# Attention, soft mixture and gated layer on one core: where the products of the score maxima stand, and when the dispatch chain runs

## The chip, the cores and the metric

One core of one Trainium2 chip runs the kernel. The metric is the device time of one execution in microseconds (us). Five engines work side by side, each on its own queue in program order: TensorE (PE; its weight loads are shown as PEld), VectorE (DVE), ScalarE (ACT), GpSimd (POOL), and SyncE (SP), which issues the DMAs. They wait for each other by semaphores.

## What is computed

```python
# attention: B=4, H=8, S=1152, D=64; queries pooled in pairs
q_pool = q.reshape(B, H, S // 2, 2, D).mean(axis=3)
scores = (1 / sqrt(D)) * q_pool @ k.T
scores -= scores.max(-1)
attn = exp(scores); attn /= attn.sum(-1) + 1e-9
out = attn @ v                       # laid out as x: 2304 tokens x 512
# soft mixture: 8 experts of 4 slots
logits = x @ phi
d = exp(logits - logits.max(0)); d /= d.sum(0) + 1e-9     # dispatch, over tokens
slot_input = d.T @ x                 # then two layers with relu per expert
c = exp(logits - logits.max(1)); c /= c.sum(1) + 1e-9     # combine, over slots
x = c @ slot_out
# gated layer: rms norm, silu(xn @ w_gate) * (xn @ w_val) @ w_out
```

All of it is in float32; the products of scores use a split of q and k into a rounded and a low part.

## The kernel before

The attention goes in 16 pairs of heads (`p`), each over nine key tiles `kt` of 128 keys, with the 576 pooled queries in two halves `h`. For one key tile and half, `qk` (lines 366 to 380) writes a score tile into PSUM with eight matmuls (high k by high q, low k by high q, high k by low q, and minus the row maxima), and ScalarE turns it into an `e` tile with an exponential. `add_e` sums the `e` tiles on GpSimd (`acc`), for the softmax's denominator. `av` multiplies by the values. The pairs 0 and 15 (`HALVED`) take their halves one after the other; the middle pairs 1 to 14 take both halves in each key tile.

The row maxima of the next pairs come from products of their own (`max_item`, lines 315 to 332): two matmuls of rounded q and k into a PSUM tile `mxp`, and a reduction on VectorE. A pair has twelve such items and two shorter ones (`max_tail`). `max_red` joins them, `max_row` transposes (`mxt`) and copies them negated (`mrow`), `send_row` moves them by DMA to `mr`, which the scores of the next pair use.

Score tiles, `mxp` tiles and all tiles of the side work share one PSUM tag with three slots of two banks (`two_banks`, line 225; `bank` takes a slot too). A tile takes a slot when the reader of an earlier tile has been written into the program and waits on the chip until that reader is done. The values' accumulators have two slots of their own.

The order of the work is written out by hand (lines 823 to 851): for each key tile, the steps of `STEP` run in turn: `q0`, `q1` are the two score tiles, `m` is one item of maxima if the quota of `MAX` allows, `e0`, `e1` are the additions, and `a`, `b`, `c` are the values' products of the three last key tiles, in every third key tile only (`VISIT`). So three key tiles of scores (a stretch) are followed by a visit to the values. The side work of the pair (roundings, low parts, the denominators of the pair before, its division, its logits, the dispatch) has due times in `AT`: the whole part is the key tile, the fraction the place among the steps. Everything goes into the engines' queues in that order.

For the pair before, `sums`, `recips`, `x_turn` (transposes `xo`, line 442), `x_divide` (line 451), `x_logits` (`xl`, line 460), `x_share` (`ls`, line 469) and `logit_add` (`lg`, lines 479, 480) give the normalized x and its logits. Four pairs make a batch: at the end of pairs 4, 8 and 12 `d_turn` transposes the batch's logits (`lgt`, line 497) and takes their maxima (`mm`, line 498), `d_exp` exponentiates them at the start of the pair behind, and `slot_part` and `slot_turn` (`pp`, line 538) follow in it. `low_k` (`kl`, line 310) and `low_q` are the low parts for the next pair, `turn_64` joins two parts of a weight, all on VectorE. After the attention come the experts and the gated layer, which the change doesn't touch.

Of the kernel before, what the change touches and what calls it, by code (L numbers as in the profile page):

```python
# [18 lines left out]
NP = 16  # L19
# [5 lines left out]
TB = 96  # L25
# [2 lines left out]
NG = 6  # L28
NF = 12

STEP = "q0 m q1 m e0 e1 a b c".split()
STEP_0 = "q m m e a b c".split()
VISIT = 3
PART = 5
MAX = [1, 1, 2, 1, 1, 2, 1, 1, 2]
MAX_1 = [2, 2, 2, 2, 2, 2, 1, 1, 2]
AHEAD = 4
AT = dict(
    take_x=0.0,
    load_64=[0.1, 3.0, 5.0],  # L40
# [1 line left out]
    load_k=0.31,  # L42
    spill=[1.4, 4.4],
    sum_q=2.2,
    sums=2.7,
    round_k=[2.72, 5.6],
    abs_64=[2.73, 8.6, 8.61],
    turn_64=[2.66, 5.63, 5.64],
    recips=2.84,
    max_tail=[2.85, 2.86],  # L50
    low_q=2.95,
    max_red=5.6,
    high_q=5.61,
    low_k=[5.65, 8.62],
    max_row=5.8,
    send_row=6.0,
    x_turn=[5.83, 8.83],
    x_divide=[5.84, 8.84],
    block_q=5.9,
    load_v=7.3,  # L60
    x_logits=8.85,
    drop_x=8.855,
    x_share=8.86,
    logit_add=8.87,
    d_turn=8.95,
    d_exp=0.05,
    d_back=2.83,
    d_copy=2.835,
    slot_part=5.82,
    slot_copy=5.95,  # L70
    slot_turn=8.82,
    c_soft=[2.97, 5.66, 8.63],
    load_ew=[1.0, 3.4],
    load_14=[0.7, 1.7, 2.2, 2.7, 3.7, 4.2, 4.7, 5.7, 6.2, 7.7],
    load_15=[0.5, 1, 1.5, 2, 2.5, 3, 3.5, 4, 4.5, 5.5, 5.84, 6, 6.5, 7, 7.5, 8, 8.5],
)
AT_0 = dict(
    round_k1=[1.06, 1.56],
    block_q1=2.6,
    low_k=[1.3, 1.8],  # L80
# [65 lines left out]
def attention_softmoe_gated_kernel(ctx: ExitStack, tc: tile.TileContext, kT, qT, vv, ip, cst, w1, w2, wg, wv, wo, rg, out):  # L146
# [291 lines left out]
    def x_turn(p, js):  # L438

        o = bank([TB, len(js), 128], "xo")  # L440
        for i, j in enumerate(js):
            pe.transpose(out=o[:, i, :], in_=xu[p][:, TB * j:TB * j + TB], identity=ident)  # L442
            xo[p, j] = o, i

    def x_divide(p, js):
        r = rr[p].rearrange("p h t s -> p (h t) s")
        o = xo.pop((p, js[0]))[0]
        for j in js[1:]:
            xo.pop((p, j))
        n, j0 = len(js), js[0]  # L450
        dv.tensor_tensor(out=xts[j0 // 3][:, j0 % 3:j0 % 3 + n, p % 4, :].rearrange("p n (s d) -> p n s d", s=2),
                         in0=o[:, 0:n].rearrange("p n (s d) -> p n s d", s=2),
                         in1=r[:, j0:j0 + n, :, None].to_broadcast([TB, n, 2, 64]), op=ALU.mult)
# [227 lines left out]
    def side(p):  # L681
# [27 lines left out]
        if l >= 0:  # L709
            at("take_x", lambda i: take_x(l))  # L710
            at("sums", lambda i: sums(l))
            at("recips", lambda i: recips(l))
            at("x_turn", lambda i: x_turn(l, range(3 * i, 3 * i + 3)))
            at("x_divide", lambda i: x_divide(l, range(3 * i, 3 * i + 3)))
            at("drop_x", lambda i: rel("B"))
            at("x_logits", lambda i: x_logits(l, range(6)))
            at("x_share", lambda i: x_share(l, range(6)))
            at("logit_add", lambda i: logit_add(l))
            if p % 4 == 0:
                at("d_turn", lambda i: dpart.__setitem__(("d", l // 4), (d_turn(l // 4), d_neg(l // 4))))  # L720
            if p % 4 == 1 and p > 1:
                b = p // 4 - 1
                at("d_exp", lambda i: d_exp(b, *dpart.pop(("d", b))))
                at("d_back", lambda i: d_back(b))
                at("d_copy", lambda i: d_copy(b))
                at("slot_part", lambda i: slot_part(b))
                at("slot_copy", lambda i: slot_copy(b))
                at("slot_turn", lambda i: slot_turn(b, pt[:, b]))
            if p % 4 == 2 and p > 2:
                b = p // 4 - 1  # L730
                at("c_soft", lambda i: (c_max, c_exp, c_soft2)[i](b))
# [26 lines left out]
    with tc.manual_schedule():  # L758
# [64 lines left out]
        for p in range(NP):  # L823
# [2 lines left out]
            steps = [(kt, h) for h in range(2) for kt in range(NKT)] if p in HALVED else [(kt, None) for kt in range(NKT)]  # L826
            for u, (kt, h) in enumerate(steps):
                now = u / 2 if p in HALVED else u
                order = STEP if h is None else STEP_0
                quota = min(sum((MAX_0 if p == 0 else MAX_1 if p == 1 else MAX)[:u + 1]),  # L830
                            0 if p == NP - 1 else 12 - AHEAD if p == NP - 2 else 99)
                for i, step in enumerate(order):
                    while todo and todo[0][0] <= now + i / len(order) / len(steps) * 9:
                        todo.pop(0)[2]()
                    n = int(step[1]) if len(step) > 1 else h
                    if step[0] == "q":
                        qk(p, kt, n)
                    elif step == "m":
                        if mx < quota:
                            next_max(p, mx)  # L840
                            mx += 1
                    elif step[0] == "e":
                        add_e(p, kt, n)
                    elif kt % VISIT == VISIT - 1:
                        k = kt - 2 + "abc".index(step)
                        for x in (0, 1) if h is None else (h,):
                            if p == NP - 1 and x == 1 and k == NKT - 1:
                                sums(p, (1,))
                            av(p, k, x)
# [411 lines left out]
```

## Time and profile before

| | us |
|---|---|
| median of 3 runs | 778.94 |
| range of the runs | 778.91 to 779.56 |
| span of the profiled execution, first to last instruction | 776.2 |
| TensorE busy in the span | 736.0 (95%) |
| VectorE / ScalarE / GpSimd busy | 477.7 / 410.5 / 426.5 |
| mean granted clock of TensorE | 0.984 |

The profiled execution is known by its span; the median of the runs, which also holds what lies around the span, is 2.7 us longer. In the rows of the profile, L375 is line 375 of the kernel; "sc<-qh,kh" names the tile written and the tiles read; "x2" merges neighbours of one kind; in brackets stands how long the engine was idle before, and what released it.

### The profile page before, as it was taken

The numbers are of one execution on the slowest core, as the hardware profiler recorded it, in microseconds if no ns is written. First come the engines' busy times: TensorE is split into PE (matmuls) and PEld (weight loads), VectorE is DVE, ScalarE is ACT, GpSimd is POOL, SyncE is SP. The second block draws the span as 40 slices with busy tenths as digits, with TensorE's granted clock in tenths as the row PEclk, the third lists the DMA queues.
The fourth block names the chain that finished last, engine by engine and source line by source line (L and its number), as shares of the span: only waits on it lengthen the run. The fifth ranks groups of instructions, "written<-read, shape, count | busy, mean of one in ns | idle before, by whom it ended". The sixth has DMA issues, their size and how long they took to land.

```text
span 776.2 us, 15539 instructions
## 1 busy us (share of the span) xinstructions
PE 736.0 (95%) x6143; PEld 508.0 (65%) x6143; DVE 477.7 (62%) x711; ACT 410.5 (53%) x809; POOL 426.5 (55%) x340
## 2 busy tenths in 40 slices
PE   5999999989999998999998999989989999999998
PEld 2556666655666665666665666644437788888887
DVE  6866787777787875678777676443125665545320
ACT  2456665655675664665664564443227675555330
POOL 5336777766777775676775666413004765445330
PEclk9999999999999998999999999997999999999999
DMA  4231543753556545245236042447995010000001
GB/s 166 92 115 61 170 147 99 237 160 111 173 165 200 173 138 200 82 147 200 81 136 228 29 140 86 164 147 253 389 380 216 0 56 14 28 27 28 28 27 41
DMA packets 52728, 103.57 MB, mean 133 GB/s; under 512 B 5816, under 2 KB 19632, under 8 KB 52656
## 3 DMA queue, kind: packets, MB, share of 16 engines
q1 hardware_dynamic: 52656, 102.59, 38.6%
q8 instruction: 48, 0.79, 0.4%
q14 instruction: 24, 0.20, 0.1%
HBM read 89.39 MB, written 13.11 MB: 132 GB/s over the span
## 4 chain that ended last, share of the span: by engine, by line
PE 84%; DVE 7%; ACT 4%; DMA 2%; issue 2%; SPq 0%; ACTq 0%; DVEq 0%
PE sc L375 21%; PE yo L1164 19%; PE av L398 18%; PE mxp L324 5%; ACT e L377 3%; PE gv L1116 3%; PE sums L418 2%; PE hin L933 2%; PE xl L460 2%; DVE mx L326 2%; PE so L956 2%; PE xo L442 1%; DMA w<-in_w_dram 1%; PE pp L538 1%; PE mxp L331 1%
## 5 line engine op out<-in xcount | busy, mean ns | idle before, releaser
L377 ACT ACTIVATE e<-sc 128x576 f32<-128x576 f32 x288 | 186.0, 651 | 139.6 <-PE sc L375 131.8
L392 POOL TENSOR_TENSOR acc<-acc,e 128x576 f32<-128x576 f32 x148 | 217.9, 1500 | 61.0 <-ACT e L377 46.5
L326 DVE TENSOR_REDUCE mx<-mxp 128x2 f32<-128x768 f32 x192 | 182.5, 957 | 71.9 <-PE mxp L324 66.9
L398 PE MATMUL av<-e,vt 128*64 128x288 f32 x1152 | 164.7, 416 | 0.0
L392 POOL TENSOR_TENSOR acc<-e 128x576 f32<-128x576 f32 x60 | 84.1, 1420 | 122.3 <-ACT e L377 122.2
L375 PE MATMUL sc<-qh,kh 64*128 64x288 f32 x576 | 105.3, 361 | 6.6 <-ACT e L377 1.7
L398 PEld LDWEIGHTS av<-e,vt 128*64 128x64 f32 x1152 | 72.6, 136 | 58.6 <-issue 22.5
L1164 PE MATMUL yo<-woh,hA 128*128 128x512 f32 (+1 forms) x312 | 98.9, 384 | 0.0
L375 PEld LDWEIGHTS sc<-qh,kh 64*128 64x128 f32 x576 | 55.6, 189 | 55.9 <-ACT e L377 24.1
L375 PE MATMUL sc<-mr,pick 64*128 64x288 f32 x576 | 87.4, 298 | 1.0 <-DMA mr<-mrow 1.0
L375 PE MATMUL sc<-qh,kl 64*128 64x288 f32 x576 | 87.2, 298 | 0.0
L375 PE MATMUL sc<-ql,kh 64*128 64x288 f32 x576 | 87.1, 298 | 0.0
L324 PE MATMUL mxp<-kh,qh 64*128 64x384 f32 x384 | 75.2, 390 | 10.5 <-ACT kh L783 5.7
L1121 DVE SCALAR_TENSOR_TENSOR th<-th,gv 128x384 f32<-128x384 f32 x72 | 39.8, 553 | 62.4 <-ACT th L1118 61.8
L1147 POOL TENSOR_TENSOR hA<-hu,hA 128x384 fp32r<-128x384 f32 x48 | 48.7, 1016 | 43.0 <-ACT hA L1146 39.3
L1164 PEld LDWEIGHTS yo<-woh,hA 128*128 128x128 f32 x312 | 57.6, 188 | 10.2 <-issue 0.7
L1164 PE MATMUL yo<-wol,hA 128*128 128x512 f32 (+1 forms) x151 | 57.8, 383 | 0.0
L1118 ACT ACTIVATE th<-gv 128x384 f32<-128x384 f32 x72 | 35.2, 488 | 42.1 <-PE gv L1116 38.3
L375 PEld LDWEIGHTS sc<-mr,pick 64*128 64x128 f32 x576 | 56.5, 191 | 1.4 <-DMA mr<-mrow 1.4
L375 PEld LDWEIGHTS sc<-qh,kl 64*128 64x128 f32 x576 | 56.6, 192 | 0.0
L375 PEld LDWEIGHTS sc<-ql,kh 64*128 64x128 f32 x576 | 56.3, 191 | 0.0
L324 PEld LDWEIGHTS mxp<-kh,qh 64*128 64x128 f32 x384 | 37.9, 195 | 25.4 <-ACT e L377 10.9
(178 smaller groups left out, 1042.6 us busy)
## 6 DMA issues: line engine op xcount, KB each, us to landing
w<-in_w_dram SPq DMA_DIRECT2D x86, 256.0 KB
w<-in_w_dram SPq DMA_DIRECT2D x21, 512.0 KB
vt<-in_vv_dram SPq DMA_DIRECT2D x16, 576.0 KB
qraw<-in_qT_dram SPq DMA_DIRECT2D x15, 576.0 KB
kraw<-in_kT_dram SPq DMA_DIRECT2D x15, 576.0 KB
away<-w SPq DMA_DIRECT2D x32, 256.0 KB
w<-away SPq DMA_DIRECT2D x32, 256.0 KB
raw<-in_wg_dram SPq DMA_DIRECT2D x12, 512.0 KB
```

The lines of the kernel that those rows point to most:

```text
L324: pe.matmul(o[:, s, 0:KC], lhsT=qh[p][r, 128 * t:128 * t + 128], rhs=kh[p][r, KC * c:KC * c + KC], start=True, stop=True)
L326: dv.reduce_max(out=to, in_=o[:, :, 0:KC], axis=AX.X)
L375: pe.matmul(o[:, s, 0:HQ], lhsT=w[r, wk], rhs=q[r, c], start=(i == 0), stop=(i == 3))
L377: ac.activation(ets[p, kt, h], o[:, :, 0:HQ], AF.Exp, scale=0.0625)
L392: eng.tensor_tensor(out=acc[p, h, j], in0=first[p, h, j] if n == 1 else acc[p, h, j], in1=e, op=ALU.add)
L398: pe.matmul(avt[p, h][64 * s:64 * s + 64, 0:HQ], lhsT=vt[p][:, kt, 64 * s:64 * s + 64], rhs=ets[p, kt, h][:, s], start=(kt == 0), stop=(kt ...
L418: pe.matmul(o[g:g + 32, :], lhsT=ones, rhs=acc[p, h, j][:, s], start=(j == 0), stop=(j == 1))
L1116: pe.matmul(o[i], lhsT=sg[n][:, 256 * i + 128 * c:256 * i + 128 * c + 128], rhs=cT[g], start=True, stop=True)
L1118: ac.activation(t, o[0], AF.Tanh, scale=0.5)
L1121: dv.scalar_tensor_tensor(out=t, in0=t, scalar=1.0, in1=o[0], op0=ALU.add, op1=ALU.mult)
L1147: gp.tensor_tensor(out=b, in0=u, in1=f(a), op=ALU.subtract)
L1164: pe.matmul(o, lhsT=x, rhs=w[:, c], start=(ft == 0 and i == 0), stop=(ft == NF - 1 and i == 2))
```

## The change

In the middle pairs, key tiles without a visit have the steps `q0 m q1 m e0 e1`, and those with one `q0 q1 m e0 e1 a m m b c m`. The quotas let all four items of a stretch run in the visit's key tile: one behind its last score tile, two behind the first product into the values, one behind the last. Maxima run five items ahead of their pair instead of four. The due times are new: `low_q`, both `low_k`, `turn_64` stand between score tiles; `x_logits` goes into the second visit, `x_share` and `logit_add` into the key tile behind it; `x_turn` transposes all six tiles at once into one slot of two banks in the third visit, `d_turn` goes just ahead of it, and `d_exp` behind the values' products of the same visit, in the pair that `d_turn` is in. Pair 15 keeps its own times.

```diff
@@ -28,13 +28,14 @@
 NG = 6
 NF = 12
 
-STEP = "q0 m q1 m e0 e1 a b c".split()
+STEP = "q0 m q1 m e0 e1".split()
+STEP_V = "q0 q1 m e0 e1 a m m b c m".split()
 STEP_0 = "q m m e a b c".split()
 VISIT = 3
 PART = 5
-MAX = [1, 1, 2, 1, 1, 2, 1, 1, 2]
-MAX_1 = [2, 2, 2, 2, 2, 2, 1, 1, 2]
-AHEAD = 4
+MAX = [0, 0, 4, 0, 0, 4, 0, 0, 4]
+MAX_1 = [2, 2, 4, 1, 0, 4, 0, 0, 4]
+AHEAD = 5
 AT = dict(
     take_x=0.0,
     load_64=[0.1, 3.0, 5.0],
@@ -42,39 +43,41 @@
     load_k=0.31,
     spill=[1.4, 4.4],
     sum_q=2.2,
+    round_k=[2.5, 5.5],
+    abs_64=[2.51, 8.5, 8.51],
+    d_back=2.68,
+    d_copy=2.69,
     sums=2.7,
-    round_k=[2.72, 5.6],
-    abs_64=[2.73, 8.6, 8.61],
-    turn_64=[2.66, 5.63, 5.64],
-    recips=2.84,
-    max_tail=[2.85, 2.86],
-    low_q=2.95,
-    max_red=5.6,
-    high_q=5.61,
-    low_k=[5.65, 8.62],
-    max_row=5.8,
+    max_tail=[2.75, 2.76],
+    recips=2.77,
+    turn_64=[0.5, 1.0, 3.3],
+    low_q=3.2,
+    high_q=5.51,
+    block_q=5.52,
+    max_red=5.65,
+    slot_part=5.66,
+    slot_copy=5.67,
+    x_logits=5.7,
+    max_row=5.83,
     send_row=6.0,
-    x_turn=[5.83, 8.83],
-    x_divide=[5.84, 8.84],
-    block_q=5.9,
+    x_share=6.05,
+    logit_add=6.06,
+    low_k=[6.1, 7.2],
     load_v=7.3,
-    x_logits=8.85,
-    drop_x=8.855,
-    x_share=8.86,
-    logit_add=8.87,
-    d_turn=8.95,
-    d_exp=0.05,
-    d_back=2.83,
-    d_copy=2.835,
-    slot_part=5.82,
-    slot_copy=5.95,
-    slot_turn=8.82,
-    c_soft=[2.97, 5.66, 8.63],
+    d_turn=8.66,
+    slot_turn=8.67,
+    x_turn=8.7,
+    x_divide=[8.71, 8.72],
+    drop_x=8.73,
+    d_exp=8.85,
+    c_soft=[3.5, 5.53, 8.96],
     load_ew=[1.0, 3.4],
     load_14=[0.7, 1.7, 2.2, 2.7, 3.7, 4.2, 4.7, 5.7, 6.2, 7.7],
     load_15=[0.5, 1, 1.5, 2, 2.5, 3, 3.5, 4, 4.5, 5.5, 5.84, 6, 6.5, 7, 7.5, 8, 8.5],
 )
 AT_0 = dict(
+    max_tail=[2.85, 2.86],
+    load_v=7.3,
     round_k1=[1.06, 1.56],
     block_q1=2.6,
     low_k=[1.3, 1.8],
@@ -442,6 +445,14 @@
             pe.transpose(out=o[:, i, :], in_=xu[p][:, TB * j:TB * j + TB], identity=ident)
             xo[p, j] = o, i
 
+    def x_turn_all(p):
+
+        o = two_banks("xo")
+        for j in range(6):
+            h, i = divmod(j, 3)
+            pe.transpose(out=o[0:TB, h, 128 * i:128 * i + 128], in_=xu[p][:, TB * j:TB * j + TB], identity=ident)
+            xo[p, j] = o[0:TB, h, 0:384].rearrange("p (n d) -> p n d", n=3), i
+
     def x_divide(p, js):
         r = rr[p].rearrange("p h t s -> p (h t) s")
         o = xo.pop((p, js[0]))[0]
@@ -710,17 +721,17 @@
             at("take_x", lambda i: take_x(l))
             at("sums", lambda i: sums(l))
             at("recips", lambda i: recips(l))
-            at("x_turn", lambda i: x_turn(l, range(3 * i, 3 * i + 3)))
+            at("x_turn", lambda i: x_turn(l, range(3 * i, 3 * i + 3)) if p == NP - 1 else x_turn_all(l))
             at("x_divide", lambda i: x_divide(l, range(3 * i, 3 * i + 3)))
             at("drop_x", lambda i: rel("B"))
             at("x_logits", lambda i: x_logits(l, range(6)))
             at("x_share", lambda i: x_share(l, range(6)))
             at("logit_add", lambda i: logit_add(l))
-            if p % 4 == 0:
+            if p % 4 == 0 and p < NP - 1:
                 at("d_turn", lambda i: dpart.__setitem__(("d", l // 4), (d_turn(l // 4), d_neg(l // 4))))
+                at("d_exp", lambda i: d_exp(l // 4, *dpart.pop(("d", l // 4))))
             if p % 4 == 1 and p > 1:
                 b = p // 4 - 1
-                at("d_exp", lambda i: d_exp(b, *dpart.pop(("d", b))))
                 at("d_back", lambda i: d_back(b))
                 at("d_copy", lambda i: d_copy(b))
                 at("slot_part", lambda i: slot_part(b))
@@ -826,7 +837,7 @@
             steps = [(kt, h) for h in range(2) for kt in range(NKT)] if p in HALVED else [(kt, None) for kt in range(NKT)]
             for u, (kt, h) in enumerate(steps):
                 now = u / 2 if p in HALVED else u
-                order = STEP if h is None else STEP_0
+                order = STEP_0 if h is not None else STEP_V if kt % VISIT == VISIT - 1 else STEP
                 quota = min(sum((MAX_0 if p == 0 else MAX_1 if p == 1 else MAX)[:u + 1]),
                             0 if p == NP - 1 else 12 - AHEAD if p == NP - 2 else 99)
                 for i, step in enumerate(order):
```

## Rows read from the trace of the kernel before

**Rows 1.** The page: chain by engine (part 4), and maxima's reductions (part 5).
```profile
PE 84%; DVE 7%; ACT 4%; DMA 2%; issue 2%; SPq 0%; ACTq 0%; DVEq 0%
...
L326 DVE TENSOR_REDUCE mx<-mxp 128x2 f32<-128x768 f32 x192 | 182.5, 957 | 71.9 <-PE mxp L324 66.9
```

**Rows 2.** The view of waits: who for whom, us in total, times, longest.
```profile
PEld sc L375 <- ACT e L377: 24.1, 75, 0.9
```

**Rows 3.** Timeline of a stretch (start us, us, engine, line, operation; idle before).
```profile
310.64 0.40 PE L375 MATMUL sc<-qh,kh 64*128 64x288 f32 x2
...
312.24 0.19 PEld L375 LDWEIGHTS sc<-qh,kh 64*128 64x128 f32 x2 [0.33 <-ACT e L377]
...
315.71 2.16 PE L398 MATMUL av<-e,vt 128*64 128x288 f32 x16
```

**Rows 4.** Timeline of the last stretch of pair 14.
```profile
477.73 0.40 PE L375 MATMUL sc<-qh,kh 64*128 64x288 f32 x2
...
478.58 3.42 ACT L377 ACTIVATE e<-sc 128x576 f32<-128x576 f32 x6 [1.92 <-PE sc L375]
...
481.15 2.16 PE L398 MATMUL av<-e,vt 128*64 128x288 f32 x16
```

**Rows 5.** Timeline: the first scores of pairs 3 and 4.
```profile
111.06 0.40 PE L375 MATMUL sc<-qh,kh 64*128 64x288 f32 x2
...
140.27 0.40 PE L375 MATMUL sc<-qh,kh 64*128 64x288 f32 x2
```

**Rows 6.** Timeline of TensorE behind a visit: the first scores and a product.
```profile
321.48 0.40 PE L375 MATMUL sc<-qh,kh 64*128 64x288 f32 x2
321.72 0.30 PE L375 MATMUL sc<-qh,kl 64*128 64x288 f32 x2
...
322.12 0.34 PE L324 MATMUL mxp<-kh,qh 64*128 64x384 f32 x2
322.30 0.30 PE L375 MATMUL sc<-qh,kh 64*128 64x288 f32 x2
```

**Rows 7.** Timeline of a second visit: the maxima's transpose and its copy.
```profile
317.80 0.33 PE L342 MATMUL mxt<-cs,mxw 128*128 128x128 f32 x1
...
318.17 0.27 ACT L344 ACTIVATE mrow<-mxt 9x128 fp32r<-9x128 f32 x1 [0.98 <-PE mxt L342]
```

**Rows 8.** Timelines of VectorE and GpSimd, pairs 3 and 14.
```profile
130.00 0.74 DVE L310 TENSOR_TENSOR kl<-kraw,kh 128x576 fp32r<-128x576 f32 x1
...
136.59 1.68 DVE L310 TENSOR_TENSOR kl<-kraw,kh 128x576 fp32r<-128x576 f32 x1
...
141.16 0.36 DVE L480 TENSOR_TENSOR lg<-lg,ls 96x192 f32<-96x192 f32 x1
...
479.31 2.81 POOL L392 TENSOR_TENSOR acc<-e 128x576 f32<-128x576 f32 x2 [3.56 <-ACT e L377]
482.08 5.62 POOL L392 TENSOR_TENSOR acc<-acc,e 128x576 f32<-128x576 f32 x4
...
485.39 1.02 DVE L479 TENSOR_TENSOR lg<-lg,ls 96x192 f32<-96x192 f32 x1
...
486.45 1.46 DVE L480 TENSOR_TENSOR lg<-lg,ls 96x192 f32<-96x192 f32 x1
```

**Rows 9.** Timeline at pair 8's end; stretches (us, busy by engine, clock, DMA).
```profile
295.49 0.41 PE L497 MATMUL lgt<-cs,lg 96*32 96x96 f32 x3 [1.31 <-DVE lg L480]
...
296.44 0.42 PE L497 MATMUL lgt<-cs,lg 96*32 96x96 f32 x3 [0.54 <-DVE mm L498]
...
296.79 0.40 PE L375 MATMUL sc<-qh,kh 64*128 64x288 f32 x2
...
304.61 1.19 PE L398 MATMUL av<-e,vt 128*64 128x288 f32 x8
...
172.17:178.30 6.13, 5.24 (x58) 3.97 (x57) 3.67 (x7) 4.07 (x10) 2.00 (x2) 1.00 0.48 177
...
297.40:304.20 6.80, 6.29 (x50) 5.46 (x48) 2.92 (x6) 4.19 (x9) 2.31 (x2) 0.50 0.37 147
```

## The prediction

> **What bounds the kernel now.** The page comes first: TensorE carries 84% of the chain that ended last [rows 1], so time can only be won where it works on something avoidable or waits. The view of waits shows the largest wait of its weight loads in the middle pairs: 24.1 us before score tiles, for ScalarE's exponentials [rows 2]. The timeline of one stretch of scores shows how: six score tiles and four products share three PSUM slots, and the first tile of a key tile waits 0.33 us for the exponential that frees its slot; the stretch lasts 5.07 us from the first score to the first matmul into the values (310.64 to 315.71) [rows 3]. The last stretch of pair 14 has no products in it: its six exponentials follow each other in 3.42 us, TensorE waits for none, and it lasts 3.42 us (477.73 to 481.15) [rows 4]. So the waits come from the products in the slots, not from ScalarE's speed. An ordinary pair takes 29.2 us (first score of pair 3 to that of pair 4) [rows 5]. Each moved piece is now checked against the queue it lands in.
>
> **Step 1, the stretches.** Three products leave each stretch and the fourth stands behind its last score. A product among scores takes 0.18 us (322.12 to 322.30) [rows 6]. A stretch with one product at its end: 3.42 + 0.18 = 3.60 instead of 5.07, so -1.47, three times: -4.4 us per pair.
>
> **Step 2, the products in the visits.** Nine products of 0.18 stand there now: +1.6. They change the matmul's shape. The first score behind matmuls into values needs 0.24 until the second (321.48, 321.72), where the next three need 0.13 each (to 322.12) [rows 6]; a product behind values pays that 0.1, and what follows it pays some at its entry. I take 0.3 per visit: +0.9. The bounds are 0 (side work makes such crossings at those places already) and 0.6 per visit. The Trainium skill (TensorEngine Tiling (Array Packing), section Key Properties) says that changing the tiling mode drains the engine, which speaks against products among values; it gives no price. With the rows' 0.1 at each of some six crossings per visit, the sum would move by no more than that 0.6.
>
> **Step 3, behind the second visit.** The raw logits' matmuls move there. Their tile is read by a VectorE step that stands behind the first score of the next stretch, so two slots serve the transposed maxima, the last product and two scores. Counting from the transpose: its scaled copy starts 0.37 later and takes 0.27 (317.80, 318.17) [rows 7], so the score that takes this slot starts at 0.69 instead of 0.45. The next score takes the product's slot: the product starts at some 0.26, its reduction some 0.49 behind (its matmul takes 0.34 and a first load 0.1 [rows 6]) and lasts 0.96 [rows 1], so at 1.75 instead of 1.33. With one more exposed load: +0.75; if slots come free in another order, 0. The logits' matmuls themselves only change place. ScalarE's side work (roundings, copies) lies behind the sixth exponential and ends ahead of the next stretch, as before: nothing; without that cover a rounding's time would come on top. Steps 1 to 3: -1.15 us per ordinary pair.
>
> **Step 4, VectorE's queue, the term that turns the sign.** Before, both halves of kl and the logit adds stand in visits, among reductions that TensorE doesn't need at once. After, the third stretch puts into VectorE's queue, behind the last product's reduction: the logits' share, two adds, kl's two halves, and only then the next product's reduction. Just there GpSimd runs six additions without a pause (479.31 to 487.70) [rows 8]. What two SBUF inputs on VectorE cost beside these: a half of kl takes 0.74 alone and 1.68 beside an addition, an add 0.36 alone. Two adds in a row, of 1.02 and 1.46, end 0.2 us behind ends of GpSimd's additions (487.91 against 487.70): the engines alternate, one instruction each [rows 8]. Counted from the maxima's transpose: reduction 0.75 to 1.70, share (a PSUM reader, 0.54) to 2.19. GpSimd's first addition is ready 1.58 behind the first score (477.73, 479.31) [rows 4, 8], at 2.27. So add 1 goes first, to 2.55; then in turn an addition to 3.81, add 2 to 4.03, 5.29, kl 5.91, 7.17, kl 7.79, and the reduction ends at 8.65. TensorE ends the third stretch at 4.8, the first values (1.1) and two products at 6.4; three unread products fill the three slots, and the six transposes of x need one: idle for 2.3 us. Behind them in TensorE's queue stand the other two products into values and the next pair's scores, and for these wait ScalarE and GpSimd. If GpSimd's addition wins the tie of 0.08 us, all is 1.35 later and the gap is 3.65. The lower bound is 0: without alternation the four operations end at 4.4, and the product's result comes at 5.0. I take 2.3, from the rows that are the very instructions. The Trainium skill (SBUF — State Buffer, section Who interferes with whom) has an instruction of VectorE with two SBUF inputs and one of GpSimd that reads SBUF exclude each other for their whole length, whichever issues first; the trace agrees, and by it both orders of the tie stay open. An ordinary pair comes to -1.15 + 2.3 = +1.15; over the twelve pairs 2 to 13: +13.8.
>
> **Step 5, the dispatch chain.** At the ends of pairs 4, 8 and 12 TensorE stood idle 1.31 us for the logits and 0.54 for the first of two maxima [rows 9]. The logits are ready early now, but that first maximum stands behind the reductions of two products, and the second transposes wait for it: some 2.45 us beside an ordinary end, against about 2.7 before: -0.2 each, -0.6. Pairs 5, 9 and 13 lose the chain's exponentials from their first stretch, 6.13 [rows 9] against 5.07 [rows 3]: -1.0; and as first of a batch they have one add instead of two: 1.48 less in step 4, of which 0.4 returns because two tiles now wait for slots; -2.1 each, -6.3. Pairs 7 and 11 get rid of divisions that held a slot at their start: an estimate of -1.3 together; pairs 6 and 10 get a subtraction ahead of a reduction that the logits' tile waits for: +1.5. Pair 1, whose stretches lose products but which gets a gap: +1.0; pair 14, without products in its last visit: -1.5. The DMA issues keep their order on SP's queue, the row of negated maxima still has a stretch and a visit until its use, and GpSimd gets no operation more: nothing; a late row would show as scores that wait for a DMA. Steps 1 to 5: 13.8 - 7.2 = +6.6 us.
>
> **Step 6, the clock.** Behind the chains of pairs 8 and 12, TensorE's granted clock went from 1.00 to 0.50 (2.4 to 1.2 GHz) for 6.8 us, behind the idle 1.31 and 0.54; behind the same chain of pair 4 it stayed at 1.00 [rows 9]. A single gap of 2.3 us is longer than these two together. I take it that the clock falls behind the ends of pairs 4, 8 and 12 and behind half of the six other pairs with a full gap. Before, the first stretch took 7.82 (296.79 to 304.61) instead of 6.13 [rows 9], 1.7 each, since half of the loss fell into waits; afterwards few waits are left there, and the loss is up to half of 6.8: I take 3.1. Six falls less the two of before (3.3): +15.3. Bounds: -3.3 and +25.
>
> **Sum.** The span of the profiled execution, 776.2, becomes 776.2 + 6.6 + 15.3 = 798.1; with the 2.7 us by which the median of the runs lies above it: 800.8.
>
> **Rivals.**
> (a) The gap comes, but the clock holds: 778.9 + 6.6 - 3.3 = 782, up to 801 with the other order of the tie. For it: the clock held behind pair 4. Against it: the gap is longer.
> (b) Faster: the alternation doesn't bite, because GpSimd's additions come later than the adds or pause between exponentials. The gap falls away in nine pairs (2.3) and in 1, 5, 9, 13 (1.2): 6.6 - 25.5 = -18.9; the two falls of the clock go too: 756.7. Its place is VectorE's queue in the third stretch; it decides from a gap of about 0.6 of the one forecast downward, where steps 1 to 5 and the saved falls outweigh it. For it: step 1 is the best-supported term. Against it: each row of two-input work beside GpSimd shows the wait.
> (c) GpSimd goes first in the tie: about 19 more, 820, with falls of the clock nearly everywhere 830. It belongs to the forecast's case.
>
> **Chances.** Forecast with (c): 0.50, its own range 790 to 832. (a): 0.20, three quarters of it slower by over 0.2%. (b): 0.24. That gains and gap cancel: 0.06. Some 0.2% (1.6 us) is what a measurement of this kernel can tell from no change. Slower: 0.50 + 0.15 + 0.03 = 0.68; same 0.06; faster 0.26. The range takes in (a), the forecast and the slower half of (b): 752 to 832.
>
> **What would show it.** Right: stretches of about 3.6 us; the reduction of the last visit's first product several microseconds behind its matmul, with kl just ahead of it at 1.4 us or more; TensorE idle before the transposes of x for that reduction; more stretches with a granted clock of 0.50. Wrong: kl at 0.75 in the third stretch, or no gap ahead of the transposes: then (b). Gaps at a clock of 1.00: then (a).

## The result and the profile after

The changed kernel takes 769.1 us (median; 768.4 to 770.4) where the kernel before takes 778.9 on the same chip: a ratio of 0.9876, interval 0.9862 to 0.989. It is 9.8 us faster; 800.8 and slower had been forecast. The time lies inside the stated range of 752 to 832, but on the other side of the kernel before, between rivals (b), 756.7, and (a), 782. The span of its profiled execution is 766.7 us, 9.5 less than before.

From the page of after: the share of the engines in the chain that ended last (part 4), and two of its larger groups (part 5):

```profile
PE 82%; DVE 9%; ACT 4%; DMA 3%; issue 2%; POOL 1%; SPq 0%; ACTq 0%; DVEq 0%
...
L329 DVE TENSOR_REDUCE mx<-mxp 128x2 f32<-128x768 f32 x192 | 178.4, 955 | 87.7 <-PE mxp L327 86.1
...
L395 POOL TENSOR_TENSOR acc<-e 128x576 f32<-128x576 f32 x60 | 109.1, 1838 | 91.1 <-ACT e L380 91.1
```

The chain is TensorE's as in [rows 1], and a reduction costs the same (955 ns, 957 before). New is the length in GpSimd's row: its additions of two `e` tiles take 1838 ns in the mean, 1420 on the page of before. Something holds them up, and that is where the forecast went wrong.

An ordinary pair, pair 3 of after: its first stretch in the view by windows (the stretch, its us, then busy us of PE, PEld, DVE, ACT, POOL, the granted clock, DMA share, GB/s), and below three more stretches, behind the ends of pairs 4, 8 and 12:

```profile
110.48:114.19 3.71, 3.71 (x52) 3.28 (x50) 3.39 (x3) 3.08 (x6) 3.71 (x3) 1.00 0.69 272
...
167.30:170.50 3.20, 3.20 (x14) 1.61 (x16) 2.10 (x4) 1.12 (x5) 2.37 (x2) 0.50 0.88 343
290.20:293.40 3.20, 3.20 (x15) 1.61 (x15) 2.44 (x6) 1.06 (x4) 2.69 (x2) 0.50 1.02 410
413.00:416.20 3.20, 3.20 (x15) 1.69 (x16) 2.12 (x5) 1.06 (x4) 2.43 (x2) 0.50 0.84 325
```

The stretch takes 3.71 us, TensorE busy throughout, where [rows 3] had 5.07. TensorE's timeline of pair 3, at the start of the third stretch and in the visit behind it up to the first score of pair 4 (start us, us, engine, line, operation; idle before):

```profile
129.18 0.33 PE L345 MATMUL mxt<-cs,mxw 128*128 128x128 f32 x1
...
130.94 0.40 PE L378 MATMUL sc<-qh,kh 64*128 64x288 f32 x2 [0.28 <-DVE mx L329]
...
133.73 0.34 PE L327 MATMUL mxp<-kh,qh 64*128 64x384 f32 x2
...
135.11 0.62 PE L327 MATMUL mxp<-kh,qh 64*128 64x384 f32 x4
135.66 0.86 PE L453 MATMUL xo<-cs,xu 128*96 128x128 f32 x6
136.45 2.16 PE L401 MATMUL av<-e,vt 128*64 128x288 f32 x16
...
138.82 0.29 PE L378 MATMUL sc<-qh,kh 64*128 64x288 f32 x2
```

The pair lasts 28.34 (110.48 to 138.82) against 29.21 in [rows 5]. The second score tile of the third stretch waits for a slot, 1.76 behind the transpose (129.18 to 130.94; 1.75 in step 3), and this stretch lasts 4.13. Nowhere in the visit does TensorE stand idle: the transposes of x at 135.66 follow the two products without the gap of 2.3 us that step 4 had put there. The waits of weight loads for exponentials before scores, 24.1 us in [rows 2], are 1.4 us in the view of waits of after.

VectorE and GpSimd at that place, timelines of after:

```profile
131.38 0.35 DVE L490 TENSOR_TENSOR lg<-lg,ls 96x192 f32<-96x192 f32 x1
131.77 1.47 DVE L491 TENSOR_TENSOR lg<-lg,ls 96x192 f32<-96x192 f32 x1
133.17 1.41 DVE L313 TENSOR_TENSOR kl<-kraw,kh 128x576 fp32r<-128x576 f32 x2
134.50 2.92 DVE L329 TENSOR_REDUCE mx<-mxp 128x2 f32<-128x768 f32 x3
...
131.44 1.59 POOL L395 TENSOR_TENSOR acc<-e 128x576 f32<-128x576 f32 x1 [3.23 <-ACT e L380]
...
132.99 2.88 POOL L395 TENSOR_TENSOR acc<-e 128x576 f32<-128x576 f32 x1
```

The queue is the one that step 4 wrote down, in its order. The first add wins the tie, by 0.06 us (131.38, 131.44; 0.08 was worked out). The second waits for GpSimd's addition, 1.47 instead of 0.35. But then both halves of `kl` follow at 0.7 each, 1.41 together, and it is GpSimd that waits: its second addition takes 2.88, twice the usual 1.42. The reduction starts at 134.50; by step 4 it was to start 7.7 behind the maxima's transpose (8.65 less 0.96), at 136.9. In the first pair of a batch, with one add, both halves of `kl` pass an addition that comes straight from a wait of 5.08 us (pair 5):

```profile
195.06 2.92 POOL L395 TENSOR_TENSOR acc<-e 128x576 f32<-128x576 f32 x1 [5.08 <-ACT e L380]
...
195.28 1.42 DVE L313 TENSOR_TENSOR kl<-kraw,kh 128x576 fp32r<-128x576 f32 x2
```

The end of a batch did not go by the forecast either. TensorE behind the third stretch of pair 4, and VectorE there, timelines of after:

```profile
164.02 0.42 PE L508 MATMUL lgt<-cs,lg 96*32 96x96 f32 x3
166.19 0.42 PE L508 MATMUL lgt<-cs,lg 96*32 96x96 f32 x3 [1.74 <-DVE mm L509]
...
167.20 3.82 PE L401 MATMUL av<-e,vt 128*64 128x288 f32 x16
...
162.87 2.92 DVE L329 TENSOR_REDUCE mx<-mxp 128x2 f32<-128x768 f32 x3
165.70 0.43 DVE L509 TENSOR_REDUCE mm<-lgt 32x1 f32<-32x288 f32 x1
```

The first maxima `mm` stand behind three reductions, the second half's transposes wait 1.74 us for them, and behind it, at the ends of all three batches, the windows above have TensorE's granted clock at 0.50, that is 1.2 of 2.4 GHz, busy throughout. Sixteen matmuls into the values take 3.82 us there and 2.16 in pair 3. The visit lasts 8.87 us (162.35 to 171.22) instead of 4.83 (133.99 to 138.82).

Pair by pair, first score to first score, before and after:

| pairs | before | after | difference |
|---|---|---|---|
| 1 | 32.66 | 32.72 | +0.1 |
| 2, 3 | 29.21, 29.21 | 28.79, 28.34 | -0.4, -0.9 |
| 6, 10 | 29.24, 29.24 | 29.05, 29.04 | -0.2, -0.2 |
| 7, 11 | 30.24, 30.23 | 29.62, 29.01 | -0.6, -1.2 |
| 4, 8, 12 (batch ends) | 31.9 each | 32.40, 32.37, 32.35 | +0.5 each |
| 5, 9, 13 (first of a batch) | 33.25, 34.9, 34.8 | 32.19, 32.14, 32.16 | -1.1, -2.8, -2.6 |
| 14 | 27.88 | 26.41 | -1.5 |

The sum is -10.0 us; the spans differ by 9.5.

### The profile page after: what moved, and what is told of

The parts are those of the page before. It is cut to its first block, busy times and chain, and to the rows that moved or that the text cites. A ratio compares the mean times of both kernels' runs of the same rounds, so it can differ in the third digit from the quotient of the medians.

```text
span 766.7 us, 15557 instructions
## 1 busy us (share of the span) xinstructions
PE 726.6 (95%) x6143; PEld 503.5 (66%) x6143; DVE 468.0 (61%) x711; ACT 396.1 (52%) x809; POOL 448.5 (59%) x340
## 4 chain that ended last, share of the span: by engine, by line
PE 82%; DVE 9%; ACT 4%; DMA 3%; issue 2%; POOL 1%; SPq 0%; ACTq 0%; DVEq 0%
PE yo L1175 19%; PE av L401 19%; PE sc L378 17%; PE mxp L327 5%; DVE mx L329 5%; PE gv L1127 3%; PE sums L421 2%; PE xl L471 2%; ACT e L380 2%; PE hin L944 2%; PE mxp L334 2%; DVE w L683 1%; PE xo L453 1%; PE so L967 1%; DMA w<-away 1%
## 5 line engine op out<-in xcount | busy, mean ns | idle before, releaser
L395 POOL TENSOR_TENSOR acc<-acc,e 128x576 f32<-128x576 f32 x148 | 215.2, 1481 | 60.9 <-ACT e L380 50.3
L380 ACT ACTIVATE e<-sc 128x576 f32<-128x576 f32 x288 | 170.2, 652 | 119.9 <-PE sc L378 118.0
L329 DVE TENSOR_REDUCE mx<-mxp 128x2 f32<-128x768 f32 x192 | 178.4, 955 | 87.7 <-PE mxp L327 86.1
L401 PE MATMUL av<-e,vt 128*64 128x288 f32 x1152 | 169.3, 425 | 0.0
L395 POOL TENSOR_TENSOR acc<-e 128x576 f32<-128x576 f32 x60 | 109.1, 1838 | 91.1 <-ACT e L380 91.1
L401 PEld LDWEIGHTS av<-e,vt 128*64 128x64 f32 x1152 | 74.5, 139 | 60.9 <-issue 26.6
L378 PE MATMUL sc<-qh,kh 64*128 64x288 f32 x576 | 95.8, 327 | 4.3 <-DVE mx L329 3.9
L327 PE MATMUL mxp<-kh,qh 64*128 64x384 f32 x384 | 70.7, 401 | 7.1 <-ACT kh L794 5.8
L327 PEld LDWEIGHTS mxp<-kh,qh 64*128 64x128 f32 x384 | 34.1, 191 | 42.9 <-ACT e L380 16.3
```

The costliest lines, as they stand in the source:

```text
L327: pe.matmul(o[:, s, 0:KC], lhsT=qh[p][r, 128 * t:128 * t + 128], rhs=kh[p][r, KC * c:KC * c + KC], start=True, stop=True)
L329: dv.reduce_max(out=to, in_=o[:, :, 0:KC], axis=AX.X)
L378: pe.matmul(o[:, s, 0:HQ], lhsT=w[r, wk], rhs=q[r, c], start=(i == 0), stop=(i == 3))
L380: ac.activation(ets[p, kt, h], o[:, :, 0:HQ], AF.Exp, scale=0.0625)
L395: eng.tensor_tensor(out=acc[p, h, j], in0=first[p, h, j] if n == 1 else acc[p, h, j], in1=e, op=ALU.add)
L401: pe.matmul(avt[p, h][64 * s:64 * s + 64, 0:HQ], lhsT=vt[p][:, kt, 64 * s:64 * s + 64], rhs=ets[p, kt, h][:, s], start=(kt == 0), stop=(kt ...
```

## The experiments

All times stand beside the kernel before on the same chip.

**Which half of the change brings the gain.** First the products at their new places, the dispatch chain at the old due times:

```diff
-    x_logits=5.7,
+    x_logits=8.85,
-    x_share=6.05,
-    logit_add=6.06,
+    x_share=8.86,
+    logit_add=8.87,
...
-    d_turn=8.66,
-    slot_turn=8.67,
-    x_turn=8.7,
-    x_divide=[8.71, 8.72],
...
-    d_exp=8.85,
+    d_turn=8.95,
+    slot_turn=8.82,
+    x_turn=[5.83, 8.83],
+    x_divide=[5.84, 8.84],
...
+    d_exp=0.05,
...
```

The lines left out put `drop_x`, the transposes in two parts and the pair of `d_exp` back in the same way; `low_q`, `low_k` and `turn_64` keep their new times.

> One part alone: products of maxima stand as in the changed kernel, but the transposes, logits and dispatch chain go back to their old due times. Theory A (the gain is the products leaving the stretches of scores): an ordinary pair stays near 28 us (three stretches of 3.7, last visit longer by the logits, 5.6), the pairs 4, 8, 12 keep the old wait at their end, and the kernel lands at 760 to 772. Rival B (the gain is the new chain: early logits, no exponentials at the start of pairs 5, 9, 13, shorter falls of the clock): close to before, 776 to 782.

It took 777.4 us, ratio 0.9974 (0.9958 to 0.999). A's range was missed. The time lies in B's, but B's reason, that the new chain brings the gain, fails in the next run. Pair 3's stretches are 4.90, 3.73 and 3.81: into the first falls the logits' work again (an add at 112.33 takes 1.22), and TensorE waits there 0.28 us for an exponential and 0.63 for a reduction. A batch ends worse than in either kernel, 9.24 to 9.38 us for the last visit. TensorE there, timeline:

```profile
171.97 0.41 PE L508 MATMUL lgt<-cs,lg 96*32 96x96 f32 x3 [1.99 <-DVE lg L491]
173.10 0.66 PE L508 MATMUL lgt<-cs,lg 96*32 96x96 f32 x3 [0.73 <-DVE mm L509]
```

Both waits of [rows 9] are back, longer (1.31 and 0.54 there), and the clock falls at all three ends. So the products alone bring 0.3%.

Then the chain at its new times, the products where they were:

```diff
-STEP = "q0 m q1 m e0 e1".split()
-STEP_V = "q0 q1 m e0 e1 a m m b c m".split()
...
-MAX = [0, 0, 4, 0, 0, 4, 0, 0, 4]
...
-AHEAD = 5
+STEP = "q0 m q1 m e0 e1 a b c".split()
+STEP_V = STEP
+MAX = [1, 1, 2, 1, 1, 2, 1, 1, 2]
...
+AHEAD = 4
```

> The other part alone: products of maxima go back between the score tiles, four pairs ahead as before; all due times of the side work stay new. Theory A: stretches return to 5 us or more, and since both halves of kl, the adds and the joins now stand between the reductions of these products, TensorE waits more than before: 780 to 800. Rival B: the chain brings the gain by itself: 767 to 774.

It took 841.6 us, ratio 1.0793 (1.0766 to 1.0821): slower, as A had it, but far outside A's 780 to 800. VectorE and TensorE in the second stretch of pair 3 (131.91 to 139.47), timelines:

```profile
133.80 1.86 DVE L307 TENSOR_TENSOR ql<-qs,qh 128x576 fp32r<-128x576 f32 x1
135.59 1.88 DVE L683 SCALAR_TENSOR_TENSOR w<-w,raw 128x512 uint32<-128x512 uint32 x1
137.39 0.94 DVE L329 TENSOR_REDUCE mx<-mxp 128x2 f32<-128x768 f32 x1
...
138.39 0.44 PE L327 MATMUL mxp<-kh,qh 64*128 64x384 f32 x2 [2.53 <-DVE mx L329]
```

`low_q` and a weight's join each wait a whole GpSimd addition, the next reduction is late, its slot is not free, and TensorE stands 2.53 us. Each of the pairs 1 to 14 has one such wait, of 2.0 to 4.0 us, and the clock falls fourteen times, in all of these pairs but pair 3 itself (twice in pair 12). These are the gap and the clock of step 4, at another place. The two halves of the change are therefore no sum: alone, one wins 2 us and the other loses 62.

**What decided step 4.** Two more adds on the logits, each reading the last one's result, in the nine pairs with a second add (the second logit part is taken off again and added again, so the logits change by rounding):

```diff
             dv.tensor_tensor(out=l, in0=l, in1=x[:, c, 1], op=ALU.add)
+            if p < NP - 2:
+                dv.tensor_tensor(out=l, in0=l, in1=x[:, c, 1], op=ALU.subtract)
+                dv.tensor_tensor(out=l, in0=l, in1=x[:, c, 1], op=ALU.add)
```

> Changed kernel plus two more two-input operations on VectorE behind the logit adds, each reading what the one before wrote (the second add taken back and made again; the result differs by rounding alone), in all pairs that have two adds and are followed by products. Theory (VectorE gives GpSimd the port only where the next operation has to wait for the one before): each takes about 1.47 instead of 0.35, the next product's reduction starts 2.9 later, TensorE gets the gap of step 4, some 2.7 us ahead of the transposes of x, in 9 pairs; the granted clock falls behind many of them: 795 to 825. Rival (VectorE keeps the port in this queue, whatever follows): each takes 0.35, 769 to 773.

It took 804.0 us, ratio 1.0297 (1.022 to 1.0375), clock 0.964. Timelines of VectorE, GpSimd and TensorE in pair 3's third stretch and behind it:

```profile
138.52 1.47 DVE L491 TENSOR_TENSOR lg<-lg,ls 96x192 f32<-96x192 f32 x1
140.02 1.47 DVE L493 TENSOR_TENSOR lg<-lg,ls 96x192 f32<-96x192 f32 x1
141.52 1.47 DVE L494 TENSOR_TENSOR lg<-lg,ls 96x192 f32<-96x192 f32 x1
142.91 1.41 DVE L313 TENSOR_TENSOR kl<-kraw,kh 128x576 fp32r<-128x576 f32 x2
...
141.23 7.07 POOL L395 TENSOR_TENSOR acc<-acc,e 128x576 f32<-128x576 f32 x4
...
145.25 1.52 PE L453 MATMUL xo<-cs,xu 128*96 128x128 f32 x6 [2.78 <-DVE mx L329]
...
177.82 0.42 PE L511 MATMUL lgt<-cs,lg 96*32 96x96 f32 x3 [2.79 <-DVE mx L329]
```

Each add that reads the one before lets one GpSimd addition through and takes 1.47; `kl` behind them again takes 1.41 for both halves. Two such waits are about what step 4 had charged to `kl` (2.9 us for 2.5): a gap of 2.77 to 2.79 us (2.3 was forecast) stands in all nine pairs, in six of them ahead of the transposes of x and at the three batch ends ahead of those of the logits (the last row, pair 4). The clock falls at every one of them, five times for 3.4 us and four times for 6.8, and the time, 799.1 to 810.8 in four executions, is near the forecast's 800.8.

The rival: that any two-input operation more would do it. One more that depends on nothing here (it doubles a half of `ls` that is not read again):

```diff
             dv.tensor_tensor(out=l, in0=l, in1=x[:, c, 1], op=ALU.add)
+            if p < NP - 2:
+                dv.tensor_tensor(out=x[:, c, 0], in0=x[:, c, 0], in1=x[:, c, 0], op=ALU.add)
```

> Changed kernel plus one more two-input operation of the same shape at the same place, which reads nothing that its neighbours write (it doubles a half of the share that is not read again). Theory (as in the run with dependent operations): it takes about 0.35 and follows the add without letting GpSimd in, kl's halves stay at 0.74, no gap: 769 to 772. Rival (the prediction's rule: every two-input operation takes turns with GpSimd's additions): 1.4 longer in 9 pairs, 779 to 790.

It took 770.1 us, ratio 0.9871 (0.9856 to 0.9886), the same as after. VectorE's timeline:

```profile
133.85 1.47 DVE L491 TENSOR_TENSOR lg<-lg,ls 96x192 f32<-96x192 f32 x1
135.25 0.34 DVE L493 TENSOR_TENSOR ls<-ls 96x192 f32<-96x192 f32 x1
135.52 1.41 DVE L313 TENSOR_TENSOR kl<-kraw,kh 128x576 fp32r<-128x576 f32 x2
```

The independent operation takes 0.34, with the same GpSimd additions beside it. At this place, then, of two operations of the same kind and size, the one that reads the result just written lets GpSimd in and the other does not. (The independent one reads one range twice; the halves of `kl`, with two different inputs, behave as it does.)

Whether this holds for other operations in that queue, and at other places, two more kernels tried. In the first, a join of a weight stands between the halves of `kl` (pairs 2, 6, 10) or ahead of them (4, 8, 12), and `low_q` behind them (3, 7, 11):

```diff
+OTHER = {(2, "turn_64"): [0.5, 1.0, 7.1], (0, "turn_64"): [0.5, 1.0, 6.08], (3, "low_q"): 7.25}
...
```

The first number of a key is the pair modulo 4; the lines left out make these times hold in the pairs 2 to 13.

> Changed kernel with other neighbours in VectorE's queue of the third stretch, by pair: pairs 2, 6, 10 have the third join of weights (a scalar_tensor_tensor) between kl's halves, pairs 4, 8, 12 have it between the logit adds and kl, pairs 3, 7, 11 have low_q right behind kl. Theory C (independence alone decides): join 0.68, kl 0.74, low_q 0.75 everywhere, GpSimd's second addition waits longer by as much. Theory D (the kind of operation decides too: a join lets GpSimd in ahead of it): the join takes some 1.9 in both places and the reduction behind comes 1.2 to 2 later; low_q behind kl stays at 0.75. Time by C: 766 to 772; by D: 772 to 785.

VectorE and GpSimd in pair 2, timelines:

```profile
107.88 0.74 DVE L314 TENSOR_TENSOR kl<-kraw,kh 128x576 fp32r<-128x576 f32 x1
108.55 0.68 DVE L684 SCALAR_TENSOR_TENSOR w<-w,raw 128x512 uint32<-128x512 uint32 x1
109.15 0.74 DVE L314 TENSOR_TENSOR kl<-kraw,kh 128x576 fp32r<-128x576 f32 x1
...
107.71 3.48 POOL L396 TENSOR_TENSOR acc<-e 128x576 f32<-128x576 f32 x1
```

Three operations in a row pass while a GpSimd addition waits (3.48 us), and in the other two orders as well; the time is 771.2 in one execution (780.1 before). C held in this queue. In the second kernel the second stretch, where `low_q` stands (93.17 below, in a stretch from 92.09 to 95.82; the expectation calls it the first), gets other operations beside it: a half of `kl` behind it (pairs 2, 6, 10), a join ahead of it (3, 7, 11), two joins behind it (4, 8, 12):

```diff
+OTHER = {(2, "low_k"): [3.25, 7.2], (3, "turn_64"): [0.5, 1.0, 3.1], (0, "turn_64"): [0.5, 3.28, 3.3]}
...
```

> Open from the runs before: behind the second logit addition of the third stretch every independent two-input operation kept the port (halves of kl 0.74 each, a join of a weight 0.68), but behind low_q in the first stretch an independent join waited for GpSimd (1.93 instead of 0.68). Here other operations stand in that place. In pairs 2, 6 and 10 the first half of kl stands between low_q and the join; in pairs 3, 7 and 11 the join stands ahead of low_q; in pairs 4, 8 and 12 a second join stands behind low_q as well. Theory E (the operation decides: a half of kl keeps the port wherever it follows another operation, a join gives it up): kl takes 0.74 behind low_q, low_q 0.74 behind a join, the join behind kl 1.9. Theory F (the place decides: in the first stretch GpSimd, which comes fresh from a wait for an exponential, gets its turn): whatever stands second there takes about 1.3 longer, kl 1.9 to 2.0, low_q 1.9 to 2.0. The time says little: 766 to 773 by either.

VectorE in pairs 2 and 3, and GpSimd in pair 2, timelines; below them, TensorE in pair 6 and the view by windows behind it:

```profile
93.17 0.75 DVE L308 TENSOR_TENSOR ql<-qs,qh 128x576 fp32r<-128x576 f32 x1
93.67 5.23 POOL L396 TENSOR_TENSOR acc<-acc,e 128x576 f32<-128x576 f32 x3 [1.92 <-ACT e L381]
93.84 1.99 DVE L314 TENSOR_TENSOR kl<-kraw,kh 128x576 fp32r<-128x576 f32 x1
95.75 1.89 DVE L684 SCALAR_TENSOR_TENSOR w<-w,raw 128x512 uint32<-128x512 uint32 x1
...
122.64 0.68 DVE L684 SCALAR_TENSOR_TENSOR w<-w,raw 128x512 uint32<-128x512 uint32 x1
123.24 1.99 DVE L308 TENSOR_TENSOR ql<-qs,qh 128x576 fp32r<-128x576 f32 x1
...
221.80 1.54 PE L472 MATMUL xl<-ipt,xu 128*96 128x64 f32 x8 [2.50 <-DVE mx L330]
...
221.40:228.10 6.70, 6.30 (x29) 3.86 (x29) 2.26 (x4) 0.00 (x0) 0.73 (x1) 0.50 0.23 74
```

What F said of the place held: here whatever stands second waits, the half of `kl` and `low_q` too, and the third waits again, although none of them reads the other's result. F's reason did not: the third waits for an addition that follows another at once, and in pair 5 of after `kl` passed one that came fresh from a wait (195.06 above). The time of the one execution, 775.7, lies above the 773 of both theories, beside 783.3 for the kernel before on that chip: in pairs 6 and 10 TensorE waits 2.50 us for a reduction, and the clock falls there for 6.8 us (pair 6 takes 33.87 us, 29.05 in after). So alternation is real in the second stretch and absent behind the logit adds in the third; independence is not the whole condition. One difference is in the rows: the GpSimd addition that waits reads `acc`, the sum so far, in the second stretch, and two `e` tiles in the third. But in the run with dependent adds `kl` passed additions of the first kind too (the second of the four at 141.23 there takes 2.85), in nine pairs. What the full condition is stays open.

**What the change left lying.** Step 3 had put 0.75 us on the slots behind the second visit. The logits' tile is freed by `x_share`; here that comes ahead of the last product of that visit:

```diff
-    x_share=6.05,
+    x_share=5.72,
```

> Changed kernel with one edit: the logits' share is due right behind the logits' matmuls, not behind the first score of the next stretch, so that their slot is free again at that score. Theory (step 3 of the prediction: two slots serve the start of the third stretch): the third stretch falls from 4.13 to about 3.72 and the wait for the negated maxima's copy goes, 0.4 to 0.65 per pair over 13 pairs: 761 to 764. Rival (VectorE's reduction of the last product is late anyway and the next score waits for it in any slot): 768 to 769.

It took 759.3 us, ratio 0.9729 (0.9709 to 0.9749), better than expected. The third stretch is 3.72 instead of 4.13, the second visit 5.46 instead of 5.60: together 0.55 in pair 3, and 0.46 to 0.57 in the other pairs of 2 to 13 that end no batch. More came from the clock, which no longer falls at the ends of pairs 4, 8 and 12: the last visit of pair 4 takes 7.22 instead of 8.87, three times 1.65. Pairs 2 to 13 together take 11.2 us less. Of this, 1.8 is lost again ahead of pair 2 in the profiled execution (its first score at 83.45 instead of 81.69), and not by the edit: pair 0 takes 34.80 us instead of 32.65, since its first twelve matmuls into the values, at 22.21, take 3.14 us where those of after, at 21.39, take 1.68, as at half the clock: the trace's records of a granted clock of 1.00 begin at 25.21 there and at 20.40 in after. In three other kernels, too, pair 0 lasts 34.7 to 34.8.

That the clock stays up is not explained by the wait before the second transposes of the logits, which is still 1.74 us. The same wait, of 1.66 to 1.75, stands at fifteen batch ends: the clock fell at three of three in after, two in the kernel with the independent operation, one in the one with other orders, none in the one with the second stretch changed and none here. Mean clocks of 0.991 to 0.993 in all four executions here, against 0.984 to 0.987 in those of after, say that this is no matter of one execution. Behind the wait at the end of pair 4 in the kernel with the independent operation, by windows:

```profile
169.00:172.40 3.40, 3.40 (x33) 2.19 (x32) 3.05 (x7) 1.86 (x6) 3.11 (x3) 1.00 1.01 390
```

VectorE's timeline here shows a further effect:

```profile
132.37 0.36 DVE L491 TENSOR_TENSOR lg<-lg,ls 96x192 f32<-96x192 f32 x1
132.65 1.42 DVE L313 TENSOR_TENSOR kl<-kraw,kh 128x576 fp32r<-128x576 f32 x2
```

The second add too, which reads the first one's result, now comes ahead of GpSimd (0.36), whose addition starts only with it; nothing in this queue waits any more.

The other repair goes to the batch ends: both halves are transposed first, then both reduced, so that TensorE need not wait for the first maximum between them:

```diff
             for t in range(3):
                 pe.transpose(out=o[i][:, TB * t:TB * t + TB], in_=lg[b][:, 3 * h + t, :], identity=ident[0:TB, 0:TB])
+        for i, h in enumerate(hs):
             dv.reduce_max(...)
```

> Changed kernel with one edit: at the ends of pairs 4, 8 and 12 the transposes of both halves of the batch's logits are issued ahead of both maxima, instead of one half, its maximum, the other half. Theory (TensorE's 1.74 us idle there is only the second half waiting behind the first half's maximum in VectorE's queue, and the granted clock of 0.50 behind it is paid for this idle): the idle and the falls of the clock at 167, 290 and 413 us go, some 3.4 us each: 758 to 762. Rival 1 (the clock falls all the same): about 764. Rival 2 (the next tile, the transposes of x, waits for the same queue): 767 to 769.

It took 760.5 us, ratio 0.9752 (0.9731 to 0.9772), as the theory had it. TensorE at the end of pair 4, timeline:

```profile
164.06 0.67 PE L508 MATMUL lgt<-cs,lg 96*32 96x96 f32 x6
165.01 0.86 PE L453 MATMUL xo<-cs,xu 128*96 128x128 f32 x6 [0.28 <-DVE mx L329]
```

The wait of 1.74 is gone, and so are the three falls of the clock; the visits last 5.78 instead of 8.87, three times 3.1 us, 9.3 in all. Both repairs together:

> Changed kernel with both edits of the two runs before: the share due right behind the logits' matmuls, and the transposes of both halves ahead of both maxima. Theory (two separate stalls of TensorE, one per pair, one in pairs 4, 8, 12): the gains add, 769.1 - 9.8 - 8.6 = 751, within 749 to 754. Rival (they overlap, since either removes the falls of the clock): 755 to 758.

It took 755.3 us, ratio 0.9679 (0.9663 to 0.9695): faster than both kernels. The two repairs alone had gained 9.8 and 8.6 on after; together they gain 13.8 (by the ratios to the kernel before, 1.5% and 1.2% alone, 2.0% together). The rival held: with either one the same three falls of the clock are gone, 1.65 us each, so their gains overlap.

## Why the prediction failed, step by step

**Steps 1 to 3 held.** Stretches of 3.60, 3.60 and 4.35 with the slots' share were forecast; 3.72, 3.72 and 4.13 came, with the rest of step 3 in the second visit. The pair was to take 28.06 without a gap and took 28.34. The visits sum to 16.77, where 16.5 was worked out, so the 0.3 us per visit for changed shapes was 0.1 too low at most.

**Step 4 failed, and with it the sign.** Its queue, its order, its tie and the first wait are in the trace. The false step is "the engines alternate, one instruction each". It was taken from two adds in a row [rows 8], of which the second reads what the first writes, and carried over to the two halves of `kl`, which read nothing of the kind: they took 0.74 us each where step 4 had 1.9 with GpSimd's turn, and the gap of 2.3 us did not come. The dependent adds of the experiment brought the gap and the falls of the clock, and with them nearly the time of the forecast; the independent one cost nothing. The row of 1.68 for one half of `kl` [rows 8] was no support for two in a row: it stands alone, behind a reduction. In the middle pairs of before, no row has two independent two-input operations in a row while an addition of GpSimd waits, so its trace could not tell. The rule is not false everywhere: in the second stretch, in after (a join behind `low_q` at 122.28 takes 1.93) as in the kernel with the products at their old places, independent operations did take turns. It was false for the queue to which it was applied; why the engines take turns in the one place and not in the other stays open. The Trainium skill (SBUF — State Buffer, section Who interferes with whom) lets issue order decide who blocks. In after GpSimd's second addition starts, by its row, at 132.99, ahead of the end of the second add (131.77 and 1.47) and of the first half of `kl`, 133.17, and yet both halves of `kl` went ahead of it, which that rule does not foresee; in the second stretch the order of the starts and the order of running do agree.

**Rival (b) was right as a mechanism, for another reason.** It expected the alternation not to bite because GpSimd would come late. GpSimd came on time, and lost. The sign that the prediction named for it, `kl` at 0.75 in the third stretch and no gap ahead of the transposes, is what the trace shows. Its 756.7 was 12.4 too low; the batch ends hold 8.6 of that, by the run that repairs them.

**Step 5 was mis-sized at the batch ends.** A batch end was to cost 2.45 us beside an ordinary one; it cost 4.04 (8.87 less 4.83). Of this 1.74 is the wait for `mm`, 1.66 the half clock (3.82 less 2.16), and the rest the transposes. Step 5 had the wait and its cause; the clock's share it left to step 6. Pairs 6 and 10 got 0.69 of their +0.75 (second visit 6.29 instead of 5.60). Pairs 7 and 11, which were to gain 1.3 together beside an ordinary pair, gained nothing beside it (-0.6 and -1.2, pair 3 -0.9); in pair 7 TensorE waits 1.19 us for a reduction ahead of the sums (239.11). The firsts of a batch were to gain 1.75 without the gap's terms (1.15 and 1.0 less 0.4). Pair 5 gained 1.1, and pairs 9 and 13 2.8 and 2.6, of which 1.7 is the fall of the clock that they had before and lost: 0.7 less than forecast each. The rows of maxima did not come late: by part 5 of the page, scores waited for a DMA 1.0 us in the whole execution.

**Step 6: the number failed, the mechanism held in part.** In after the clock does fall at the ends of pairs 4, 8 and 12, in all three, for 3.4 us each and not 6.8, so each costs 1.66 us and not 3.1; the three other falls had no gap to follow. The wait alone does not give this, and the guess had luck in it: the same wait left the clock up at nine of the fifteen batch ends counted above. In the run with dependent adds, where gaps of 2.8 exist, nine of nine brought a fall, more than the half that was taken. Of rival (a), that gaps of this length leave the clock alone, little is left: of 25 gaps of 2.0 to 4.0 us in three kernels (nine there, fourteen with the products at their old places, two with the second stretch changed) one, of 2.53, left it up.

**The sum.** The gaps' 25.5 us (nine of 2.3, four of 1.2) did not come, nor half of the falls; the batch ends cost more than was forecast, with the clock. The run with dependent adds, 804.0, shows that the price put on the gap was about right, in part by luck (nine falls instead of six, and no gaps in the four pairs of 1.2); the gap was not there.

## What to carry to other kernels

A row that shows two operations taking turns with another engine proves it only for operations that stand in the same relation: check whether the second one reads the first one's result, and look for a row at the very place, before the price is carried over. On a queue that has to hand a slot back, put the two-input work where the other engine has nothing to run, as the early share did here. And where an edit takes away the longest wait, look at what now ends the stage: here one step that freed a slot late and one reduction between two transposes held more (13.8 us) than the change itself had gained (9.8).

## What the runs showed of the hardware

- A GpSimd addition of 1.4 us can wait behind several independent two-input operations of VectorE: 2.9 us with two halves of `kl` ahead of it, 3.5 with a join as well; in another stretch the same kinds of operation are let through only in turn with GpSimd's additions (1.9 to 2.0 each instead of 0.7). Which condition tells the two apart was not settled.
- Waits of TensorE of 1.66 to 1.75 us at a batch end went with a clock of 0.50 in six of fifteen cases: at all three ends of after, and at none with the early share, where the wait is the same. With gaps of 2.8 it fell in nine of nine, with gaps of 2.0 to 4.0 in the pairs of the kernel with the products at their old places in thirteen of fourteen. A gap's row alone does not yet tell.
- Of two profiled executions, one had its first twelve matmuls into the values in 3.14 us and the other in 1.68; the records of a granted clock of 1.00 begin at 25.21 us in the one and at 20.40 in the other, and pair 0 took 2.2 us longer in the one.
- Behind a batch end of after, 3.4 us at half the clock cost 1.66 us of time (3.82 less 2.16 for sixteen matmuls into the values).
